# Numerators of linear attention that read the turned rows in storage order, with tokens put in order at the PSUM evacuation and units 8 to 31 begun four steps earlier

## The chip, the core and the metric

One core of a Trainium2 chip runs the whole kernel. The core has five engines with a queue of instructions each: TensorE (PE in the profile; its weight loads are listed as PEld), VectorE (DVE), ScalarE (ACT), GpSimd (POOL) and SyncE (SP), which here only starts transfers. Each engine works through its queue in order, and semaphores let one engine wait for another. SBUF is the working memory, PSUM the memory that TensorE writes its results to, in eight banks.

The metric is device time in microseconds, the median of three runs. All numbers of single instructions come from one profiled execution.

## What is computed

A transformer block on 2048 tokens of width 1024: linear attention with 32 heads of 32 features, then a ReLU MLP of width 3584, both with a layer norm ahead and a residual.

```
pq = einsum(q, w_phi);  pk = einsum(k, w_phi)            # per head, 32 x 32
phi_q = concat(softmax(pq), softmax(-pq));  phi_k likewise   # 64 features
kv  = einsum("bhsf,bhsd->bhfd", phi_k, v)                # 64 x 32 per head
z   = einsum("bhsf->bhf", phi_k)
num = einsum("bhqf,bhfd->bhqd", phi_q, kv)
den = einsum("bhqf,bhf->bhq", phi_q, z) + 1e-6
h   = x + (num / den) @ wo
out = h + relu(layernorm(h) @ w1) @ w2
```

The change lies in `num`, the numerators.

## The kernel before

Everything is float32. The large products split each operand into a high and a low part and take three matmuls (`mm3`, L182 to L184). One such triple is a **step**. Steps are grouped into **items** of eight: a projection of one tile of 128 tokens to 512 columns. Other work is hung on the steps by hand: `when(step, f, ...)` writes the instructions of `f` into the queues right behind that step of TensorE. So the order within each queue is the order of the steps, whatever the engine is doing by then. The splits of weights (`Units.advance`: a copy on ScalarE, L125, then a subtraction on GpSimd or VectorE, L129) go in behind each step when a buffer of the ring is free; the transfers that fetch the weights are queued on SP with them.

The items run in this order: keys and values of the first half of the tokens, queries of the first half, keys and values of the second half (`last_kv` is the last of these), queries of the second half (16 items), then the output projection `wo` (32 items, four groups of tokens), then the MLP. The attention itself runs beside the last queries and the output projection.

**Units.** The queries' exponentials are stored to DRAM (`ed`) and come back as 32 units. A unit is a tile of 128 partitions by 1024 values and holds 256 tokens for a part of the heads. A unit goes through these functions, each at its own offset from the unit's `start`:

- `at_load` (L552, queued on SP): fetches the rows into a `qe` tile, one of six buffers. The buffer is that of the unit six before, whose last reader is that unit's burst of numerators.
- `at_sums` (L595, GpSimd, twice) and `at_reduce` (L602, VectorE, twice): products with `z` and their sums.
- `at_cross` (L613, ScalarE, four small copies), `at_den` (L617 and L618, GpSimd), `at_inverse` (L621, VectorE): the denominators.
- `at_scale` (L631; L626 for the first six units; GpSimd): the rows are divided in place.
- `at_turn` (L637, VectorE): a transpose of every 32 x 32 block in place, so that the features come to lie on the partitions.
- `at_num` (L650, TensorE; on odd units, for two units together): a **burst** of 16 products, each of 64 features by 32 columns of `kvL` with 256 tokens, into two PSUM banks `ac`. The profile lists two matmuls per product. There are 16 bursts.
- right behind it the evacuation: two copies on ScalarE (L657) give the high part of `oT`, and two steps later `at_low` (L667, two subtractions on VectorE) gives the low part. `oT` is the stationary operand of the output projection.

Units 0 to 5 have their denominators made ahead (`early_*`), and only load, scale, turn and numerators at the normal place. Units below 8 are spaced 19/2 steps apart and begin at step 8 (last_kv + 4); from unit 8 on they are 8 steps apart, one unit per item.

After `at_turn` a tile's free dimension is ordered (i, n, c, t): two halves, four blocks `n`, four heads' places `c`, 32 tokens `t`. The token order wanted in `oT` is t outside and n inside. In the kernel before, the matmul's moving operand is read in that order: n innermost, 128 elements apart, then t, then i. What lands in PSUM is then in order and the evacuation reads neighbours.

In the same queues beside the units: the queries' maxima, differences and sums on VectorE (L516, L517, L520, L521, L534, L535), one set per query item; the residual additions (L704, L707) of the output projection; layer-norm statistics (L222, L765); and the splits of `wo` (`w` and `wf` for the two sets of buffers).

Of the kernel before, what the change touches and what calls it, by code (L numbers as in the profile page):

```python
# [140 lines left out]
def kernel(  # L141
# [416 lines left out]
    e_q, ez_of, tz_of, den_of, ph_of, acc_of, phT_of = {}, {}, {}, {}, {}, {}, {}  # L558
# [75 lines left out]
    def at_turn(u):  # L634

        ph = ph_of.pop(u)
        v.transpose(ph, ph)  # L637
        phT_of[u] = ph.rearrange("p (i n c t) -> p c i t n", i=2, n=4, c=4)

    def at_num(u):  # L640


        acc_of[u] = banks = ac_bank(), ac_bank()
        for j in range(2):
            b, q, r = UNITS[u - 1 + j]
            for g in range(2):
                rows = slice(64 * g, 64 * (g + 1))
                for c in range(4):
                    h = 2 * c + r
                    pe.matmul(banks[g][32 * c:32 * (c + 1), 256 * j:256 * (j + 1)],  # L650
                              kvL[rows, 2 * q + h // 4, 32 * (h % 4):32 * (h % 4 + 1)],
                              phT_of[u - 1 + j][rows, c], start=j == 0, stop=j == 1)
        del phT_of[u - 1], phT_of[u]
        if u % 8 == 1:
            oT[b] = opool[b % 2].tile([P, 2, 8, 512], F32R, name="oT")
        for g in range(2):
            act.activation(at_out(u, 0, g), at_in(banks[g]), AF.Copy)  # L657

    def at_in(ps):
        return ps.rearrange("p (u i n) -> p u i n", u=2, i=2)  # L660

    def at_out(u, part, g):
        return oT[u // 8][:, part, u % 8 - 1:u % 8 + 1, :].rearrange("p u (i g n) -> p u i g n", i=2, g=2)[:, :, :, g]

    def at_low(u):
        for g, ps in enumerate(acc_of.pop(u)):
            v.tensor_sub(at_out(u, 1, g), at_in(ps), f32(at_out(u, 0, g)))  # L667

    oT, opool = {}, {}
# [277 lines left out]
    def item(gen, *args, keys):  # L947
        items.append((gen, args + (keys,)))
        steps.extend((k,) for k in keys)
        return len(items) - 1  # L950
# [11 lines left out]
    for b, tiles in enumerate(groups):  # L962
        for hf in range(2):

            pairs = b == 0 and hf == 0
            for j in range(0, 4, 2 if pairs else 1):
# [3 lines left out]
                for half in range(2):  # L970
                    n = item(wo_pair, tiles[j:j + 2], hf, half, keys=[("wo", hf, 4 * half + k // 2) for k in range(8)])
# [26 lines left out]
    def when(step, f, *args):  # L998

        if step < 8 * first_up:  # L1000
            do(step // 8, step % 8, f, *args)
        else:
            do(first_up + (step - 8 * first_up) // 4, step % 4, f, *args)
# [4 lines left out]
    for t in range(1, NT):  # L1008
        n = t - 1 if t < HT else q_n[1, t - HT] + 1
# [42 lines left out]
    last_kv = kv_n[1, 3, NT - 1]  # L1052
# [62 lines left out]
    a0 = last_kv + 6  # L1115
    for (sl, t), n in q_n.items():
# [3 lines left out]
        b, i = place_of[t]  # L1120
# [1 line left out]
            when(8 * n + 34, sm_store, b)  # L1122
            when(8 * n + (48, 48, 48, 72)[b], sm_load, b)
    for u in range(32):
        start = 8 * (a0 + u) if u >= 8 else 8 * (last_kv + 4) + 19 * u // 2
        slack = 6 if u < 6 else 0

        for step, f, *args in ((-5, at_load), (6, at_sums, 0), (10, at_reduce, 0), (9, at_sums, 1), (12, at_reduce, 1),
                               (14, at_cross), (16, at_den), (18, at_inverse), (20, at_scale), (26, at_turn)):
            if u >= EARLY or f in (at_load, at_scale, at_turn):  # L1130
                when(max(start + step, 8 * (last_kv + 4)), f, u, *args)
        if u % 2:
            when(start + 30 + slack, at_num, u)
            when(start + 32 + slack, at_low, u)
        if u < EARLY:
            start = 8 * (kv_n[1, u // 2, NT - 1] + 4) + (-2, 19)[u % 2]
            for step, f in ((0, early_load), (9, early_sums), (14, early_reduce), (17, at_cross), (20, at_den), (22, early_scale)):
                when(start + step, f, u)
# [35 lines left out]
    def up_step(b, p, m):  # L1174

        return up0 + 4 * (up_n[b, p, m] + 1 - first_up)

    for j, m in enumerate(UP):

        for g in range(2):  # L1180
            step = up0 + (8 * j + (-62, -29)[g] if j < 4 else 6 * (j - 4) + 4 + 2 * g)
# [4 lines left out]
            step = up_step(0, NP - 1, m) + 2 * j  # L1186
# [4 lines left out]
    for b in range(2):  # L1191
        for p in range(NP):
            for m, k, f, *args in UP_BESIDE:
                if f is up_store:
                    args = [b, p, *args]
# [7 lines left out]
    for n, (w, p, j) in enumerate((w, p, j) for w in (1, 2) for p in range(NP) for j in range(2)):  # L1203
        step = sums_at[n]
# [7 lines left out]
    for b in range(2):  # L1212
        for m in DOWN:
            n = down_n[b, m, NP - 1] + 1
# [110 lines left out]
```

## Time and profile before

| | |
|---|---|
| median of three runs | 1884.09 us (1883.66 to 1885.63) |
| profiled execution | 1884.29 us, span 1882.5 us |
| TensorE busy | 1871.4 us, 99% of the span |
| VectorE, GpSimd, ScalarE busy | 1067.8, 979.9, 770.9 us |
| granted TensorE clock | 1.0 |
| L650, all bursts | 33.8 us busy, 512 matmuls |
| first and last burst begin at | 551.0 and 763.2 us |

How the rows are read: a row of a group names the line, the engine, the operation, output and inputs by the program's tile names, the shape, and the count. Times in a time line are microseconds from the start of the span, first the start, then the length. Behind a bar stand busy time, the mean of one in ns, and the idle time of the engine just before it with the engine and line that ended it. Matmuls overlap, and their ends are modelled, so the distance between their starts says more than their length. A row with a `64*32` names the rows and columns of the array that the matmul uses.

### The profile page before, as it was taken

The page shows a single profiled execution, that of the slowest core. Times are in us where ns is not written, and L with a number is a line of the kernel's source. Part 1 is how long each engine was busy: PE and PEld are TensorE (multiplying, and loading weights), DVE is VectorE, ACT ScalarE, POOL GpSimd, SP SyncE. Part 2 cuts the span into 40 slices and gives each one's busy share as a digit, 9 for nine tenths or more (in the row PEclk, how much of TensorE's full clock was granted, in tenths as well). Part 3 has the DMA queues.
Part 4 walks back from the last instruction along what each step waited for, and adds up shares of the span by engine and source line. Part 5 has one row for each costly group of instructions (what it writes and reads, how often), then busy time and mean ns, then how long its engine had stood idle before and what let it go on. Part 6 is the DMA issues. An engine that isn't in the chain of part 4 may idle for free.

```text
span 1882.5 us, 28853 instructions
## 1 busy us (share of the span) xinstructions
PE 1871.4 (99%) x10064; PEld 1516.4 (81%) x10064; DVE 1067.8 (57%) x1655; ACT 770.9 (41%) x1379; POOL 979.9 (52%) x991
## 2 busy tenths in 40 slices
PE   9999999999999999999999999999999999999999
PEld 7777788888876677888888888888888888888887
DVE  7787688677689777565555563444433333343333
ACT  5322244233333334355455554444444444444442
POOL 4877745888846979343233222222344444444443
PEclk9999999999999999999999999999999999999999
DMA  7988798666575766787889985666677677767775
GB/s 225 291 284 294 230 292 268 204 192 200 181 222 178 228 222 190 242 288 213 260 256 261 318 275 176 192 191 216 212 236 216 207 226 237 239 214 217 217 215 177
DMA packets 333635, 433.04 MB, mean 230 GB/s; under 512 B 28720, under 2 KB 194608, under 8 KB 333488
## 3 DMA queue, kind: packets, MB, share of 16 engines
q1 hardware_dynamic: 299696, 414.41, 70.2%
q10 hardware_dynamic: 33792, 16.78, 3.1%
q8 instruction: 79, 1.29, 0.3%
q14 instruction: 68, 0.56, 0.1%
HBM read 293.21 MB, written 137.89 MB: 229 GB/s over the span
## 4 chain that ended last, share of the span: by engine, by line
PE 97%; POOL 1%; DVE 1%; issue 0%; DMA 0%; ACT 0%; SPq 0%; DVEq 0%; POOLq 0%
PE mm L182 25%; PE mm L183 25%; PE mm L184 25%; PE ac L182 4%; PE ac L184 4%; PE ac L183 4%; PE tp L184 2%; PE tp L183 2%; PE tp L182 2%; PE ac L650 2%; PE tp L246 1%; PE ac L465 1%; POOL ez L595 0%; PE tp L291 0%; POOL w L129 0%
## 5 line engine op out<-in xcount | busy, mean ns | idle before, releaser
L129 POOL TENSOR_TENSOR w<-raw,w 128x512 fp32r<-128x512 f32 x353 | 469.1, 1331 | 702.3 <-ACT w L125 665.1
L125 ACT ACTIVATE w<-raw 128x512 fp32r<-128x512 f32 x686 | 408.8, 626 | 508.8 <-PE mm L184 235.1
L129 DVE TENSOR_TENSOR w<-raw,w 128x512 fp32r<-128x512 f32 x333 | 271.0, 814 | 513.4 <-ACT w L125 504.8
L182 PE MATMUL mm<-w,xT 128*128 128x512 f32 x768 | 305.4, 398 | 0.0
L183 PE MATMUL mm<-w,xT 128*128 128x512 f32 x768 | 299.8, 390 | 0.4 <-POOL w L401 0.4
L184 PE MATMUL mm<-w,xT 128*128 128x512 f32 x768 | 299.2, 390 | 0.0
L184 PE MATMUL mm<-hT,w 128*128 128x512 f32 x672 | 261.4, 389 | 0.0
L182 PE MATMUL mm<-hT,w 128*128 128x512 f32 x672 | 261.4, 389 | 0.0
L183 PE MATMUL mm<-hT,w 128*128 128x512 f32 x672 | 261.4, 389 | 0.0
L182 PEld LDWEIGHTS mm<-w,xT 128*128 128x128 f32 x768 | 144.1, 188 | 36.7 <-issue 5.5
L363 POOL TENSOR_TENSOR b<-b 128x256 f32<-128x256 f32 x176 | 144.3, 820 | 48.6 <-DMA b<-in_w_dram 37.6
L184 PEld LDWEIGHTS mm<-w,xT 128*128 128x128 f32 x768 | 144.2, 188 | 30.7
L183 PEld LDWEIGHTS mm<-w,xT 128*128 128x128 f32 x768 | 144.3, 188 | 29.2 <-POOL w L401 1.0
L182 PE MATMUL mm<-w 128*128 128x512 f32 x392 | 152.5, 389 | 0.0
L183 PE MATMUL mm<-w 128*128 128x512 f32 x392 | 152.5, 389 | 0.0
L184 PE MATMUL mm<-w 128*128 128x512 f32 x392 | 152.5, 389 | 0.0
L182 PEld LDWEIGHTS mm<-hT,w 128*128 128x128 f32 x672 | 126.1, 188 | 26.3
L183 PEld LDWEIGHTS mm<-hT,w 128*128 128x128 f32 x672 | 126.1, 188 | 26.2
L184 PEld LDWEIGHTS mm<-hT,w 128*128 128x128 f32 x672 | 126.1, 188 | 26.1
L454 POOL TENSOR_TENSOR zacc<-zacc,kphi 128x512 f32<-128x512 f32 x60 | 80.7, 1345 | 10.1 <-DVE kphi L446 10.1
L182 PEld LDWEIGHTS mm<-w 128*128 128x128 f32 x392 | 73.6, 188 | 15.3
L183 PEld LDWEIGHTS mm<-w 128*128 128x128 f32 x392 | 73.6, 188 | 15.3
(173 smaller groups left out, 3119.8 us busy)
## 6 DMA issues: line engine op xcount, KB each, us to landing
raw<-t SPq DMA_DIRECT2D x224, 256.0 KB, 3.8
raw<-ad SPq DMA_DIRECT2D x196, 256.0 KB, 3.0
raw<-in_w_dram SPq DMA_DIRECT2D x168, 256.0 KB, 3.1
ad<-c SPq DMA_DIRECT2D x112, 256.0 KB, 3.6
b<-in_w_dram SPq DMA_DIRECT2D x44, 512.0 KB, 5.5
t<-b SPq DMA_DIRECT2D x44, 512.0 KB, 5.0
ad<-s SPq DMA_DIRECT2D x84, 256.0 KB, 4.0
ed<-qe ACTq DMA_DIRECT2D x64, 256.0 KB, 3.9
```

Of the source, the lines that this page charges most:

```text
L125: nc.scalar.activation(w[:, 0, :], raw[1], AF.Copy)
L129: eng.tensor_tensor(out=w[:, 1, :], in0=raw[1], in1=w[:, 0, :].bitcast(F32), op=ALU.subtract)
L182: pe.matmul(ps, a_hi, b_hi, start=first, stop=False, skip_group_check=more)
L183: pe.matmul(ps, a_hi, b_lo, start=False, stop=False, skip_group_check=more)
L184: pe.matmul(ps, a_lo, b_hi, start=False, stop=last, skip_group_check=more)
L246: pe.transpose(pt[:, k, :], xn[:, (4 * j + k) * P:(4 * j + k + 1) * P], ident)
L363: pool.tensor_tensor(out=tsum[*u, *out], in0=tsum[*u, *a], in1=tsum[*u, *b], op=ALU.subtract)
L454: pool.tensor_tensor(out=zacc[s], in0=zacc[s], in1=phi_of[key], op=ALU.add)
L465: pe.matmul(kv_ps[s][g][32 * i:32 * (i + 1), 0:64], vt[:, 32 * h:32 * (h + 1)], phi[:, 64 * h:64 * (h + 1)], start=first, stop=last)
L650: pe.matmul(banks[g][32 * c:32 * (c + 1), 256 * j:256 * (j + 1)], kvL[rows, 2 * q + h // 4, 32 * (h % 4):32 * (h % 4 + 1)], phT_of[u - 1 + ...
```

## The change

Three things, all in the attention:

1. `at_turn` hands the numerators a view in which the moving operand is read with the 32 tokens `t` innermost, next to each other, and the eight blocks (i and n together) outside, 128 apart. The product's columns then land in PSUM in the order (i, n, t).
2. `at_in` and `at_out`, used by the copies (L657) and the subtractions (L667), read PSUM with n innermost, 32 elements apart, and write `oT` in the order it had before: four blocks by 32 tokens, contiguous runs of 128. What `oT` holds is the same.
3. The start of units 8 to 31 is four steps lower. Their numerators and evacuation get a slack of four, so they stay at the same step. `at_load` moves from 5 to 8 steps ahead of the start, for all units (the earliest ones are held by the lower limit of the schedule).

```diff
         v.transpose(ph, ph)
-        phT_of[u] = ph.rearrange("p (i n c t) -> p c i t n", i=2, n=4, c=4)
+        phT_of[u] = ph.rearrange("p (n c t) -> p c n t", n=8, c=4)
...
     def at_in(ps):
-        return ps.rearrange("p (u i n) -> p u i n", u=2, i=2)
+        return ps.rearrange("p (m n t) -> p m t n", m=4, n=4)
 
     def at_out(u, part, g):
-        return oT[u // 8][:, part, u % 8 - 1:u % 8 + 1, :].rearrange("p u (i g n) -> p u i g n", i=2, g=2)[:, :, :, g]
+        return oT[u // 8][:, part, u % 8 - 1:u % 8 + 1, :].rearrange("p u (i g t n) -> p g (u i) t n", i=2, g=2, n=4)[:, g]
...
     for u in range(32):
-        start = 8 * (a0 + u) if u >= 8 else 8 * (last_kv + 4) + 19 * u // 2
-        slack = 6 if u < 6 else 0
+        start = 8 * (a0 + u) - 4 if u >= 8 else 8 * (last_kv + 4) + 19 * u // 2
+        slack = 6 if u < 6 else 4 if u >= 8 else 0
 
-        for step, f, *args in ((-5, at_load), (6, at_sums, 0), (10, at_reduce, 0), (9, at_sums, 1), (12, at_reduce, 1),
+        for step, f, *args in ((-8, at_load), (6, at_sums, 0), (10, at_reduce, 0), (9, at_sums, 1), (12, at_reduce, 1),
                                (14, at_cross), (16, at_den), (18, at_inverse), (20, at_scale), (26, at_turn)):
```

## The prediction

> **What bounds the kernel.** I read the page first, then TensorE's waits, then the line that the change rewrites, then the queues of VectorE and GpSimd around it.
>
> ```profile
> span 1882.5 us, 28853 instructions
> PE 1871.4 (99%) x10064; PEld 1516.4 (81%) x10064; DVE 1067.8 (57%) x1655; ACT 770.9 (41%) x1379; POOL 979.9 (52%) x991
> PE 97%; POOL 1%; DVE 1%; issue 0%; DMA 0%; ACT 0%; SPq 0%; DVEq 0%; POOLq 0%
> ```
>
> TensorE is busy for 99% of the span, and 97% of the chain that ended last runs through it. So a microsecond counts only if TensorE's own work shrinks, or one of its few waits goes or comes.
>
> ```profile
> PE ac L650 <- DVE qe L637: 1.9, 1, 1.9
> PE mm L183 <- DVE w L129: 1.1, 1, 1.1
> ```
>
> These two waits lie in the attention stage. The first is a burst of numerators (L650) that waits for the turned rows of its second unit; the second is an output projection that waits for a split weight. The change has two handles, then: what a burst costs on TensorE, and when the turned rows are ready.
>
> **What a burst costs.** Sixteen bursts run, one per pair of units. The rows give shortest, median and longest ns of a matmul by line.
>
> ```profile
> L650 PE MATMUL ac<-qe,kvL x512: 610/627/707, 551.0 to 764.7; 64*32 64x256 f32 x171
> L291 PE MATMUL mm<-wt,wphi x224: 371/374/398, 40.3 to 200.5; 32*32 32x256 f32 x112
> ```
>
> Both stream 256 float32 columns through small tiles of the array. L650 reads its moving rows with the four blocks `n` innermost, 128 elements apart; L291, in the weight fold, reads eight runs of 32 neighbours, 128 apart. That is exactly the pattern that L650 has after the change. It takes 374 ns against 627. A burst and a fold in order of time (start, length, group):
>
> ```profile
> 550.42 0.39 PE L183 MATMUL mm<-w,xT 128*128 128x512 f32 x1
> 550.65 0.39 PE L184 MATMUL mm<-w,xT 128*128 128x512 f32 x1
> 550.97 0.71 PE L650 MATMUL ac<-qe,kvL 64*32 64x256 f32 x8
> 551.44 0.71 PE L650 MATMUL ac<-qe,kvL 64*32 64x256 f32 x8
> 551.89 0.70 PE L650 MATMUL ac<-qe,kvL 64*32 64x256 f32 x8
> 552.33 0.70 PE L650 MATMUL ac<-qe,kvL 64*32 64x256 f32 x8
> 552.96 0.50 PE L182 MATMUL mm<-w,xT 128*128 128x512 f32 x1
> ...
> 199.38 0.45 PE L291 MATMUL tp<-wt,wphi 32*32 32x256 f32 x8
> 199.62 0.42 PE L291 MATMUL tp<-wt,wphi 32*32 32x256 f32 x8
> 200.03 0.50 PE L291 MATMUL tp<-wt,wphi 32*32 32x256 f32 x8
> ```
>
> L650 goes in four rounds of eight tiles, 0.45 us apart (550.97, 551.44, 551.89, 552.33), and the next projection starts 0.63 after the last: 1.99 in all. The fold's second round of the same tiles starts 0.24 after the first. With that spacing three rounds take 0.72; the last one shortens by the difference of the durations, 0.63 - 0.25 = 0.38. A burst then takes 1.10 and saves 0.89 us. Bounds: the fold's third round comes 0.41 after its second (200.03 - 199.62), where it goes to other weights and other columns; with one such step, at the change from one unit to the next, a burst saves only 0.72. At best rounds follow like the projection's matmuls, 0.23 apart: 0.92. I take 0.89, because L650's rounds before show no longer step at that place (0.45 like the others). Sixteen bursts: 14.2 us (11.5 to 14.7). The 0.32 between a projection and a burst (550.65 to 550.97) stays.
>
> **Evacuation.** Each burst is copied out by two ScalarE and two VectorE instructions. They now read PSUM in steps of 32 elements and write runs of 128; no row of before reads PSUM so.
>
> ```profile
> L657 ACT ACTIVATE oT<-ac x32: 590/596/601, 553.1 to 765.8; 128x512 fp32r<-128x512 f32 x32
> L667 DVE TENSOR_TENSOR oT<-ac,oT x32: 628/681/694, 554.3 to 766.6; 128x512 fp32r<-128x512 f32 x32
> L637 DVE STREAM_TRANSPOSE qe<-qe 128x1024 f32<-128x1024 f32 x32 | 39.2, 1224 | 4.3 <-POOL qe L626 2.4 <-POOL qe L631 1.8
> L781 DVE STREAM_TRANSPOSE y<-xin 128x1024 f32<-128x1024 f32 x4 | 8.1, 2031 | 1.2 <-DMA raw<-t 1.2
> ```
>
> The nearest row of a stepped access on VectorE is L781, a transpose that writes every fourth element: 2031 ns against 1224 for L637, which writes neighbours, 1.66 times. TensorE's own ratio is 627/374 = 1.68. Lower bound: no change, since writes stay in runs and reads were at their best. I take no change. A fold round gives 256 float32 columns in 0.24 us, 0.94 ns each, twice the 0.45 of a projection's column (0.23 for 512), as if TensorE streamed each column twice. A stepped round of 0.45 us is then 0.9 ns a read, while L667 takes 681/512 = 1.33 ns an element, so a stepped read need not be its limit. (If each column is read only once, a stepped read is 1.8 ns, and the upper end is near.) Upper end: 1.66 times, 0.45 us more per instruction.
>
> [...]
>
> **Who covers what.** From unit 8 on, all that a unit issues moves four steps up, 4 x 0.68 = 2.7 us (a step is three matmuls 0.23 apart): on GpSimd two products, two denominator steps and the scaling; on VectorE two sums, a reciprocal and the turn; on ScalarE four small copies. The row load moves seven steps up (three for earlier units). Numerators and evacuation stay in place. In stretches (busy us and count of PE, PEld, DVE, ACT, POOL, then clock and DMA):
>
> ```profile
> 565.00:581.00 16.00, 16.00 (x95) 11.91 (x93) 15.76 (x26) 5.18 (x13) 9.96 (x13) 1.00 0.58 180
> 581.00:592.00 11.00, 11.00 (x72) 7.80 (x71) 10.68 (x17) 3.21 (x4) 6.72 (x10) 1.00 0.44 126
> 592.00:611.00 19.00, 17.87 (x100) 12.78 (x99) 17.18 (x27) 8.34 (x19) 15.14 (x17) 1.00 0.65 197
> 624.00:640.00 16.00, 14.13 (x90) 9.50 (x97) 13.24 (x18) 6.01 (x18) 15.84 (x14) 1.00 0.67 216
> 681.00:707.00 26.00, 26.00 (x161) 18.91 (x160) 19.57 (x30) 6.56 (x21) 19.20 (x22) 1.00 0.82 263
> ```
>
> VectorE is 98% full from 565 to 592, GpSimd 99% from 624 to 640; by 681 both have a quarter free. So the seven bursts up to 641 gain only what these queues let through, and the nine behind keep theirs: 9 x 0.89 = 8.0 us.
>
> The first seven, in order. The fourth burst (units 6 and 7):
>
> ```profile
> 590.88 1.19 DVE L637 STREAM_TRANSPOSE qe<-qe 128x1024 f32<-128x1024 f32 x1
> 591.99 0.64 DVE L602 TENSOR_REDUCE qtz<-ez 128x16 f32<-128x512 f32 x1
> ...
> 592.38 2.08 PE L650 MATMUL ac<-qe,kvL 64*32 64x256 f32 x32
> ```
>
> Unit 7's turn ends at 592.07, in a full queue that faster reads don't shorten, and unit 8's second sum (0.6) now stands ahead of it: 592.67. TensorE comes 3 x 0.89 = 2.67 sooner, at 589.71, and wants unit 7 two rounds later, at 590.19. It waits 2.5 us. What is kept: 4 x 0.89 - 2.5 = 1.06.
>
> ```profile
> 610.38 0.50 PE L183 MATMUL mm<-w,oT 128*128 128x512 f32 x1 [1.13 <-DVE w L129]
> ...
> 624.37 1.18 PE L650 MATMUL ac<-qe,kvL 64*32 64x256 f32 x16
> 627.42 1.21 PE L650 MATMUL ac<-qe,kvL 64*32 64x256 f32 x16 [1.87 <-DVE qe L637]
> ...
> 630.81 1.30 POOL L129 TENSOR_TENSOR wf<-raw,wf 128x512 fp32r<-128x512 f32 x1
> 633.46 0.39 PE L182 MATMUL mm<-wf,oT 128*128 128x512 f32 x1
> ```
>
> The projection's wait of 1.13 at 610: a sum of unit 10 (0.6) moves ahead of the split on VectorE and TensorE comes 1.06 sooner, up to 2.8 if the queue doesn't move, nothing if it does; I leave it at 1.13. The fifth burst adds 0.89: 1.95. The sixth (units 10, 11) starts its second half at 627.42 instead of 624.37 + 0.92, a wait of 2.13. TensorE gets there 1.95 + 0.44 = 2.39 sooner, so unit 11 would have to be 4.5 sooner; four steps give 2.7, and 1.8 of wait remains. Kept: 1.95 + 0.89 + 2.13 - 1.8 = 3.2. Then the split that GpSimd ends at 632.11 is wanted at 633.46, 1.35 later; with TensorE 3.2 sooner and one more unit product ahead of it (1.3, the length of this split) the wait lies between nothing and 3.1; I take half, 1.6. With the seventh burst 1.6 + 0.89 = 2.5 us is kept at 641.
>
> **The row load.**
>
> ```profile
> SPq L552 <- PE ac L650: 36.6, 9, 13.1
> ...
> DMA to landing us min/median/max: 2.6/5.2/6.9
> ```
>
> From unit 14 on an even unit's load stands two steps ahead of the burst that frees its buffer, so SP waits there about 2 x 0.68 + 1.1 us, with loads and stores of the residual behind it that have more than ten steps to their use. SP waits like this already (36.6 us, nine times) with no wait on TensorE. The data is wanted 14 steps, 9.5 us, after the load's place; 2.5 + 5.2 fits, 2.5 + 6.9 is right at it and would cost GpSimd, which has room there. Nothing.
>
> **Sum.** 8.0 + 2.5 = 10.5 us. The profiled execution took 1884.29 us (0.2 over the median of the three runs, 1884.09): 1873.8.
>
> **Rivals.**
> 1. *The queues don't hold TensorE*: the loads and splits that they wait for also come sooner, all bursts keep 0.89 and both waits go: 14.2 + 1.1 + 2.1 = 17.4, 1866.9. For it: GpSimd has 3.9 us idle between 592 and 611. Against it: VectorE at 98%.
> 2. *Stepped PSUM reads are slow, 1.66 times*: 0.9 us more on VectorE per burst. It hurts where that queue is full, behind six of the first seven bursts: 5.4 lost, 1879.2. [...]
> 3. *They are so slow that VectorE sets the pace*, the other side. It decides where 12 instructions eat 10.5 us, 0.88 each, from 2.3 times on. At three times (2.04 us) they add 12 x 1.36 = 16.3: 5.8 slower, 1890.1. Nothing in before excludes it; no row shows more than 1.68.
> 4. *The reads are no faster*, because the burst's pace has another cause (two row groups in one bank pair, say): only the sixth burst's 2.1 goes, 0.6 comes back at a split: 1882.8, no measurable change. Against it: the row of L291.
>
> **Chances.** Forecast 0.58, rival 1 0.09, rival 2 0.15, rival 4 0.07, rival 3 0.11. So faster by over 0.2% (3.8 us, about what a measurement here can tell) 0.82, within it 0.07, slower 0.11. The range leaves out rivals 3 and 4: 1867 from rival 1 to 1880.5 just past rival 2. The forecast's own range is 1870 to 1877.5: from two thirds of rival 1's extra kept, to nothing kept before 641 and bursts that save only 0.72.
>
> **What would show it.** L650's median near 374 ns and a burst without a wait at 1.1 us from its first matmul to the next projection: the reads. L657 and L667 still at 596 and 681 ns: the evacuation. A wait of TensorE on L637 at the fourth burst, the sixth burst's wait smaller, waits on splits (L129) near 610 and 632: the queues. Bursts from 652 on without waits, in 13.1 - 0.9 us from one to the next: the kept gain. I would be wrong if L667 grows, if waits show up behind 652, or if L650 stays above 600 ns.

## The result and the profile after

The kernel with the change takes 1872.29 us (median of four runs, 1870.48 to 1872.47), the kernel before 1884.07 beside it. The ratio is 0.9934 with the interval 0.9917 to 0.9951: 11.8 us faster. The profiled execution of after is the shortest of the four, 1870.48 us. It is some 1.8 us better than the other three, and the stages below add up to its time, not to the median; the experiment on the loads takes that difference up.

The page of after, first lines and the chain by engine:

```profile
span 1868.7 us, 28840 instructions
PE 1856.5 (99%) x10064; PEld 1516.3 (81%) x10064; DVE 1063.8 (57%) x1655; ACT 770.5 (41%) x1379; POOL 979.0 (52%) x991
...
PE 93%; DVE 3%; POOL 1%; issue 1%; ACT 0%; DMA 0%; SPq 0%; ACTq 0%; DVEq 0%; POOLq 0%
```

TensorE is still busy 99% of the span, 14.9 us less in sum (1871.4 - 1856.5). The chain has 3% of VectorE in it where before had 1%: some of its new waits run through VectorE's queue. The changed lines, by line (shortest, median, longest ns):

```profile
L650 PE MATMUL ac<-qe,kvL x512: 375/376/632, 550.5 to 751.1; 64*32 64x256 f32 x171
L657 ACT ACTIVATE oT<-ac x32: 579/596/619, 551.7 to 752.0; 128x512 fp32r<-128x512 f32 x32
L667 DVE TENSOR_TENSOR oT<-ac,oT x32: 622/676/693, 553.5 to 752.8; 128x512 fp32r<-128x512 f32 x32
```

A matmul of the numerators went from 627 to 376 ns, and the two evacuation instructions stayed what they were (596 against 596, 676 against 681). The first burst in order of time:

```profile
550.48 1.09 PE L650 MATMUL ac<-qe,kvL 64*32 64x256 f32 x32
551.50 0.50 PE L182 MATMUL mm<-w,xT 128*128 128x512 f32 x1
```

From its first matmul to the next projection it takes 551.50 - 550.48 = 1.02 us, where before took 1.99: 0.97 saved. All bursts but the fourth and the sixth take 1.02 to 1.03.

To see where the gain is kept, I set the same burst's times in the two traces beside each other and took away the 0.49 us by which the first burst begins sooner (551.0 and 550.48 from the start of each span, before anything of the change acts).

| TensorE ahead of before, us | predicted | measured |
|---|---|---|
| after the third burst | 2.67 | 3.00 |
| after the fourth | 1.06 | 0.91 |
| ahead of the fifth | 1.06 | 1.45 |
| after the fifth | 1.95 | 2.64 |
| after the sixth | (3.2) | 5.14 |
| ahead of the seventh (behind the wait on the split) | 1.6 | 3.34 |
| after the seventh | 2.5 | 4.41 |
| after the sixteenth | 10.5 | 13.31 |

TensorE's waits in the attention stage of after (total, times, longest), and the two smaller ones in order of time, at the sixth burst and at the split of GpSimd:

```profile
PE ac L650 <- DVE qe L637: 2.8, 2, 2.4
...
PE mm L183 <- POOL wf L129: 1.5, 1, 1.5
```

```profile
622.35 0.67 PE L650 MATMUL ac<-qe,kvL 64*32 64x256 f32 x16 [0.45 <-DVE qe L637]
...
629.73 0.50 PE L183 MATMUL mm<-wf,oT 128*128 128x512 f32 x1 [1.46 <-POOL wf L129]
```

The largest is at the fourth burst, in order of time:

```profile
588.90 0.66 PE L650 MATMUL ac<-qe,kvL 64*32 64x256 f32 x16
591.94 1.11 PE L650 MATMUL ac<-qe,kvL 64*32 64x256 f32 x16 [2.38 <-DVE qe L637]
592.98 0.80 PE L182 MATMUL mm<-w,xT 128*128 128x512 f32 x1
593.57 0.63 PE L183 MATMUL mm<-w,xT 128*128 128x512 f32 x1
594.00 0.63 PE L184 MATMUL mm<-w,xT 128*128 128x512 f32 x1
```

The first half runs, the second waits for unit 7's turn. VectorE meanwhile:

```profile
588.59 0.68 DVE L602 TENSOR_REDUCE qtz<-ez 128x16 f32<-128x512 f32 x1
589.18 1.21 DVE L534 TENSOR_REDUCE qsm<-qe 128x32 f32<-128x1024 f32 x1
590.43 0.35 DVE L535 RECIPROCAL qsm<-qsm 128x32 f32<-128x32 f32 x1
590.70 1.19 DVE L637 STREAM_TRANSPOSE qe<-qe 128x1024 f32<-128x1024 f32 x1
```

It has no gap: a sum of unit 8 (L602, moved up), a query item's sum, then the turn, which ends at 591.89. TensorE starts again at 591.94. Something follows that I had not foreseen. The projections behind come 0.43 us apart (593.57 to 594.00) instead of 0.23. The stretches behind the wait (busy us and count of PE, PEld, DVE, ACT, POOL, then granted clock, DMA share, GB/s):

```profile
591.00:593.00 2.00, 1.06 (x17) 0.25 (x17) 2.00 (x4) 0.33 (x1) 1.87 (x2) 0.65 0.37 101
593.00:595.00 2.00, 2.00 (x12) 1.61 (x6) 2.00 (x5) 1.60 (x3) 1.41 (x2) 0.50 0.60 161
595.00:597.00 2.00, 2.00 (x10) 1.63 (x9) 2.00 (x5) 1.26 (x5) 2.00 (x2) 0.99 0.00 0
```

The granted clock is 0.50 until 595 (I call this half clock below). The burst's second half takes 1.04 us to the next projection (592.98 - 591.94) where it takes 0.57 in the first burst, and from 592.98 to 594.85 the projections run at half pace: 0.47 + 0.94, about 1.4 us lost beside the wait itself.

### The profile page after: what moved, and what is told of

Its sections match the earlier page's. It is cut to its first block, busy times and chain, and to the rows that moved or that the text cites. A ratio compares the mean times of both kernels' runs of the same rounds, so it can differ in the third digit from the quotient of the medians.

```text
span 1868.7 us, 28840 instructions
## 1 busy us (share of the span) xinstructions
PE 1856.5 (99%) x10064; PEld 1516.3 (81%) x10064; DVE 1063.8 (57%) x1655; ACT 770.5 (41%) x1379; POOL 979.0 (52%) x991
## 3 DMA queue, kind: packets, MB, share of 16 engines
q8 instruction: 79, 1.29, 0.3%
## 4 chain that ended last, share of the span: by engine, by line
PE 93%; DVE 3%; POOL 1%; issue 1%; ACT 0%; DMA 0%; SPq 0%; ACTq 0%; DVEq 0%; POOLq 0%
PE mm L182 24%; PE mm L183 24%; PE mm L184 24%; PE ac L182 4%; PE ac L184 4%; PE ac L183 4%; PE tp L184 2%; PE tp L183 2%; PE tp L182 2%; PE tp L246 1%; PE ac L465 1%; PE ac L650 1%; DVE qsm L534 0%; DVE qe L637 0%; POOL w L129 0%
## 5 line engine op out<-in xcount | busy, mean ns | idle before, releaser
L125 ACT ACTIVATE w<-raw 128x512 fp32r<-128x512 f32 x686 | 409.4, 626 | 508.8 <-PE mm L184 232.4
L183 PEld LDWEIGHTS mm<-w 128*128 128x128 f32 x392 | 73.6, 188 | 15.3
L184 PEld LDWEIGHTS mm<-w 128*128 128x128 f32 x392 | 73.6, 188 | 15.2
L182 PEld LDWEIGHTS mm<-w 128*128 128x128 f32 x392 | 73.6, 188 | 15.3
```

Of the source, the lines that this page charges most:

```text
L125: nc.scalar.activation(w[:, 0, :], raw[1], AF.Copy)
L182: pe.matmul(ps, a_hi, b_hi, start=first, stop=False, skip_group_check=more)
L183: pe.matmul(ps, a_hi, b_lo, start=False, stop=False, skip_group_check=more)
L184: pe.matmul(ps, a_lo, b_hi, start=False, stop=last, skip_group_check=more)
```

## The experiments

Theory: faster reads save about 0.97 us a burst; what is lost of it before 641 is lost to VectorE's full queue (fourth burst) and GpSimd's (sixth burst, split). Rivals: the units begun sooner bring the gain; a better order of the queues would bring the lost part back; the stepped PSUM reads or the moved loads cost something.

**The reads alone.** Units and loads at the steps of before.

```diff
-        start = 8 * (a0 + u) - 4 if u >= 8 else 8 * (last_kv + 4) + 19 * u // 2
-        slack = 6 if u < 6 else 4 if u >= 8 else 0
+        start = 8 * (a0 + u) if u >= 8 else 8 * (last_kv + 4) + 19 * u // 2
+        slack = 6 if u < 6 else 0
...
-        for step, f, *args in ((-8, at_load), (6, at_sums, 0), (10, at_reduce, 0), (9, at_sums, 1), (12, at_reduce, 1),
+        for step, f, *args in ((-5, at_load), (6, at_sums, 0), (10, at_reduce, 0), (9, at_sums, 1), (12, at_reduce, 1),
```

> Parts one and two alone: the numerators read runs of 32 and the evacuation puts the tokens in order, all units at their old steps and loads. Theory (the queues of VectorE and GpSimd hold TensorE up to 641): a burst without a wait takes 1.02 us as after the change, 16 x 0.97 = 15.5 us less work, but unit 11 and the units about it are no sooner, so the sixth burst waits longer than its 2.1 us of before, and the fourth, fifth or seventh wait too; 6 to 8 us faster, 1876 to 1878. Rival (the shorter bursts are the whole gain, the four steps do nothing): 1872, waits as after the change.

Measured: 1875.48 us against 1884.81, ratio 0.9953 (0.9939 to 0.9968). That is 9.3 us faster where 6 to 8 was expected, half a microsecond below the expected times; in the trace TensorE ends 8.6 us ahead. The waits that came up:

```profile
PE ac L650 <- DVE qe L637: 3.1, 4, 1.3
PE ac L650 <- POOL ez L595: 1.8, 1, 1.8
PE mm L183 <- DVE w L129: 1.8, 1, 1.8
```

Five bursts wait (the fourth takes 3.10 us, the fifth 1.87, the sixth 2.51, the seventh 2.10, the fourteenth 1.87). The split's wait of 1.8, just ahead of the fifth burst, is followed by half clock too, from 611.6 to 615. Without the earlier units the faster TensorE waits at five bursts, but most of the gain is the reads'.

**The earlier units alone.** The kernel before with the start, slack and load step of after.

```diff
-        start = 8 * (a0 + u) if u >= 8 else 8 * (last_kv + 4) + 19 * u // 2
-        slack = 6 if u < 6 else 0
+        start = 8 * (a0 + u) - 4 if u >= 8 else 8 * (last_kv + 4) + 19 * u // 2
+        slack = 6 if u < 6 else 4 if u >= 8 else 0
```

> Part three alone: units from the ninth on four steps sooner and the loads sooner, reads and evacuation as before. Theory: only the sixth burst's wait of 2.1 us goes and the fourth or a split gives back some tenths: 1 to 2.5 us faster, 1881.5 to 1883, no change that can be measured; bursts stay at 1.99 us. Rival (the earlier start is what frees the attention stage): at least 4 us faster, under 1880.

Measured: 1881.64, ratio 0.9983 (0.9973 to 0.9992), 3.2 us faster; 3.0 in the trace. More than the 1 to 2.5 that was expected, because not only the sixth burst's wait is gone but the projection's at 610 as well. Bursts take 1.98 to 2.03 throughout, and one wait comes in:

```profile
PE mm L183 <- POOL wf L129: 0.7, 1, 0.7
```

So this part is worth a third of the other. Both alone give 8.6 + 3.0 = 11.6 in the traces and 12.5 in the medians, together 13.3 and 11.8. So nothing large comes from doing both together.

**The fourth burst six steps later.** If the fourth burst's wait of 2.5 us is a loss by order alone, then asking for units 6 and 7 six steps later should bring it back.

```diff
-        slack = 6 if u < 6 else 4 if u >= 8 else 0
+        slack = 6 if u < 8 else 4
```

> The changed kernel with the numerators of units 6 and 7 (the fourth burst) six steps later. Theory: the burst finds its turned rows, so its wait of 2.5 us and the half clock behind it (about 1 us) go, but VectorE is as full as it was, so the weight splits of the first output projections (near 600 to 608) come no sooner and TensorE waits there instead, 2 to 3.5 us: 1870 to 1872.5. Rival (the wait at the fourth burst is a cost by itself): 3.5 us under the changed kernel, about 1868.7, no new waits near 600 to 608.

Measured: 1873.18, ratio 0.9938 (0.9924 to 0.9953), 0.9 us slower than after and 0.7 above the expected range. The fourth burst waits no more and takes 1.03 us. But the projections behind it do:

```profile
603.29 0.50 PE L183 MATMUL mm<-w,oT 128*128 128x512 f32 x1 [0.77 <-DVE w L129]
606.28 0.50 PE L184 MATMUL mm<-w,oT 128*128 128x512 f32 x1 [1.11 <-DVE oT L667]
609.11 0.80 PE L182 MATMUL mm<-w,oT 128*128 128x512 f32 x1 [1.63 <-ACT w L125]
610.90 0.80 PE L183 MATMUL mm<-w,oT 128*128 128x512 f32 x1 [1.00 <-DVE w L129]
```

Four waits, 4.5 us where 2 to 3.5 was expected, and half clock for 6.8 us from 609. Three of them are for VectorE, one for a copy on ScalarE. So this order doesn't bring the loss back: TensorE meets the work that VectorE still owes at the next things that it needs. One order is not all orders. VectorE stands idle here for 1.45 us at 600, behind a ScalarE copy (L125), so a better order may exist; none was tried.

**Less work on VectorE.** The maximum and the minimum over a query item (L516, L517) read 8 of the 32 features for the second half of the tokens; the softmax stays the same, only its guard against large exponents is weaker.

```diff
+        part = pq[:, :, 0:8] if t >= HT else pq
-        v.tensor_reduce(out=m[:, 0, :], in_=pq, op=ALU.max, axis=AX.X)
-        v.tensor_reduce(out=m[:, 1, :], in_=pq, op=ALU.min, axis=AX.X)
+        v.tensor_reduce(out=m[:, 0, :], in_=part, op=ALU.max, axis=AX.X)
+        v.tensor_reduce(out=m[:, 1, :], in_=part, op=ALU.min, axis=AX.X)
```

> The changed kernel with VectorE relieved: the maximum and minimum that shift the query softmax are taken over 8 of the 32 features for the tokens of the second half (the softmax is the same in exact arithmetic, only less guarded against overflow), about 0.35 us less for each of two reductions, 0.7 us per query item, over 5 us by the fourth burst. Theory (VectorE's full queue holds the fourth burst and the first splits): the wait at the fourth burst falls under 0.3 us, the clock stays at 1.0 behind it, and 3 us or more are gained: 1866 to 1869.5. Rival (GpSimd's products and scalings hold the turned rows, or the loads do): the wait stays at 2 us or more, and the time within 1 us of the changed kernel.

Measured: 1867.33, ratio 0.9907 (0.9893 to 0.9922), 5.0 us faster than after (3.6 in the traces, where after's is its short execution). The groups of one of the two reductions (busy, mean ns, idle before) and the stretch in which after waited and ran at half clock:

```profile
L517 DVE TENSOR_REDUCE qmx<-mm 128x16 f32<-128x512 f32 x16 | 10.9, 682 | 8.1 <-PE mm L184 8.1
L517 DVE TENSOR_REDUCE qmx<-mm 128x16 f32<-128x128 f32 x16 | 4.5, 283 | 9.8 <-PE mm L184 9.8
```

```profile
588.00:596.00 8.00, 8.00 (x63) 5.83 (x62) 7.93 (x15) 5.94 (x13) 7.26 (x10) 1.00 0.35 102
```

Each query item costs VectorE 0.8 us less (twice 682 - 283 ns). The fourth burst takes 1.08 us, TensorE is busy all 8 us, and the clock stays at 1.00: without the wait there is no half clock here. TensorE is 3.91 ahead after the fourth burst and 5.39 ahead of the fifth, where after had 0.91 and 1.45. The difference of 3.0 at the fourth burst is the wait of 2.56 (the third round of products at 591.94 instead of 589.14 + 0.24) and 0.47 of the clock. The one of 3.9 ahead of the fifth holds the other 0.94.

**Moving rows at steps of 1, 2, 4, 8, 16 and 128, burst by burst.** After, with other orders of the matmul's reads, and the PSUM reads of before.

```diff
-        phT_of[u] = ph.rearrange("p (n c t) -> p c n t", n=8, c=4)
+        k = (1, 2, 4, 8, 16, 32)[u // 2 % 6]
+        phT_of[u] = ph.rearrange("p (i n c t) -> p c i t n", i=2, n=4, c=4) if k == 32 else \
+            ph.rearrange("p (n c b a) -> p c n a b", n=8, c=4, a=k)
```

> The changed kernel with the moving rows of the numerators read in other orders, the burst deciding: the innermost elements lie 1, 2, 4, 8 or 16 apart (then the rest of each run of 32, then the blocks), and in every sixth burst 128 apart as before the change; the evacuation reads neighbours as before, so tokens come out in another order (what is left out is the ordering of the tokens). [...] Rival that any step costs: 2 is as slow as 128. Rival that only long distances cost (other banks or rows of the memory): 2, 4, 8 and 16 stay near 376 ns. Evacuation: ScalarE 596 and VectorE 676 to 681 ns as with the stepped reads of the changed kernel.

Measured in one execution (1876.03 us). Bursts in order of time, at steps of 2, 8, 16, 128 and 1:

```profile
648.29 1.17 PE L652 MATMUL ac<-qe,kvL 64*32 64x256 f32 x32
...
675.43 2.04 PE L652 MATMUL ac<-qe,kvL 64*32 64x256 f32 x32
688.50 1.30 PE L652 MATMUL ac<-qe,kvL 64*32 64x256 f32 x32
700.84 2.06 PE L652 MATMUL ac<-qe,kvL 64*32 64x256 f32 x32
715.77 1.09 PE L652 MATMUL ac<-qe,kvL 64*32 64x256 f32 x32
```

| innermost step (elements) | places read in turn | matmul, median ns | burst to next projection, us |
|---|---|---|---|
| 1 | 32 neighbours | 376 | 1.02 |
| 2 | 16, then the 16 between | 392 | 1.10 |
| 4 | 8 | 634 | 2.00 |
| 8 | 4 | 632 | 1.97 |
| 16 | 2 | 429 | 1.23 |
| 128 (before) | 4 | 622 | 1.99 |

So the pace depends on the read order, the only thing that differs between these bursts (rival 4 would have had them all alike). It falls into two groups, and not by the length of the step: 4, 8 and 128 are slow (622 to 634 ns), 2 is fast (392), and 16 is nearly as fast (429), where the reads go to and fro between two places 64 bytes apart. Both rivals of this expectation fall: not every step costs (392 ns at 2 against 622 at 128), and not only long distances do (634 and 632 ns at 4 and 8). What makes an order slow, the runs don't say.

The evacuation of this kernel, which reads neighbours in PSUM:

```profile
L659 ACT ACTIVATE oT<-ac 128x512 fp32r<-128x512 f32 x32 | 17.4, 595 | 37.0 <-PE ac L652 37.0
L669 DVE TENSOR_TENSOR oT<-ac,oT 128x512 fp32r<-128x512 f32 x32 | 20.3, 675 | 7.7 <-ACT oT L659 7.6
```

Means of 595 and 675 ns with neighbours, 596 and 673 with steps of 32 elements in after: these stepped PSUM reads cost the two engines nothing.

**What slow evacuations would have cost.** Rival 2's price, put on VectorE by hand: each subtraction of the evacuation is done twice, 1.2 us more per burst.

```diff
-            v.tensor_sub(at_out(u, 1, g), at_in(ps), f32(at_out(u, 0, g)))
+            for _ in range(2):
+                v.tensor_sub(at_out(u, 1, g), at_in(ps), f32(at_out(u, 0, g)))
```

> The changed kernel with each VectorE subtraction of the evacuation done twice (same result), 1.2 us more on VectorE per burst: what a slow read of PSUM would have cost. Theory (the queue is full behind six of the first seven bursts and has room later): 6 x 1.2 = 7.2 us lost at the most, 1877 to 1880, lost before 641, none after. Rival (VectorE sets the pace throughout): 16 x 1.2 = 19 us lost, 1891. Rival (VectorE's fullness costs TensorE nothing): 1872 to 1873.

Measured: 1879.1, ratio 0.997 (0.9958 to 0.9982), 6.8 us slower than after. The two traces lie further apart, 8.5 us at the last burst. Of this 6.9 is lost up to the end of the seventh burst (2.46 behind before, where after was 4.41 ahead), nearly all at one place: the fourth burst takes 7.08 us instead of 4.08, and 3.2 more go on the way to the fifth, where half clock lasts twice as long (to 599.6) and two splits are waited for (0.7 and 1.3).

```profile
594.99 1.11 PE L650 MATMUL ac<-qe,kvL 64*32 64x256 f32 x16 [5.37 <-DVE qe L637]
```

Most of the rest, 1.5, is lost between the fourteenth and the fifteenth burst, where none was expected: TensorE waits 1.29 us there for a layer-norm copy on ScalarE (L248). The doubled subtractions as its cause are not shown; a smaller wait of the same kind comes and goes in other variants.

**The loads back at their old steps.** After, with the row loads as many steps ahead of their use as in before.

```diff
-        for step, f, *args in ((-8, at_load), (6, at_sums, 0), (10, at_reduce, 0), (9, at_sums, 1), (12, at_reduce, 1),
+        for step, f, *args in ((-1 if u >= 8 else -5, at_load), (6, at_sums, 0), (10, at_reduce, 0), (9, at_sums, 1), (12, at_reduce, 1),
```

> The changed kernel with the row loads of all units back at the steps of before (units from the ninth on still start four steps sooner). Theory (loads are never what a unit waits for here): the time of the changed kernel within 1 us. Rival (the earlier loads carry the gain of the earlier start): GpSimd waits for rows and 2 us or more are lost, 1874.5 or more.

Measured: 1872.43, ratio 0.9935 (0.992 to 0.995), the median of after. So the place of the loads is worth nothing that these runs can show. This kernel's profiled execution (1872.08) shows what the three other runs of after may look like, since the profiled one of after was 1.6 us shorter than this. The fourth burst waits the same (2.38 in both rows), but the half clock lies later:

```profile
593.00:595.00 2.00, 2.00 (x8) 1.53 (x7) 2.00 (x5) 1.25 (x3) 1.85 (x2) 0.63 0.60 162
595.00:597.00 2.00, 2.00 (x7) 1.56 (x6) 2.00 (x5) 1.25 (x5) 2.00 (x4) 0.52 0.25 13
```

It costs about the same, but in after it began at 591.6 and so covered the burst's second half, here it began behind it, at 593.5. So here the evacuation copies on ScalarE start 0.43 us sooner (592.65 against 593.08), the weight copy behind them too, and GpSimd's queue, in the same order, runs up to 0.46 sooner. Then the same split on VectorE takes twice as long. VectorE and GpSimd around 598, in after and in this kernel:

```profile
598.27 0.63 DVE L129 TENSOR_TENSOR w<-raw,w 128x512 fp32r<-128x512 f32 x1
598.17 1.87 POOL L595 TENSOR_TENSOR ez<-qe,zb 128x512 f32<-128x512 f32 x1
```

```profile
598.28 1.28 DVE L129 TENSOR_TENSOR w<-raw,w 128x512 fp32r<-128x512 f32 x1
597.71 1.30 POOL L595 TENSOR_TENSOR ez<-qe,zb 128x512 f32<-128x512 f32 x1
598.97 1.74 POOL L129 TENSOR_TENSOR w<-raw,w 128x512 fp32r<-128x512 f32 x1
```

In after the split keeps its 0.63 and GpSimd's product takes 1.87 instead of 1.30, 0.57 longer, though its start is recorded 0.10 sooner than the split's (times on GpSimd are rough). In this kernel the product is under way, the split takes 1.28, and its end, 599.56, is 0.55 behind the product's at 599.01, as if it had waited for it. Then GpSimd's next split takes 1.74, 0.45 over its usual 1.29. The other four VectorE splits up to 610 (600.75 and 606.51 in after, 601.42 and 608.14 here) also start while a GpSimd instruction runs and end 0.54 to 0.56 behind it. That one of the two engines is served and the other waits is my reading of these lengths; no row shows a cause, and the starts of the first pair, 0.10 us apart, don't settle which came first. The three splits on VectorE from 598 to 610 take 0.63 + 1.11 + 0.75 = 2.49 us in after, 1.28 + 2.07 + 1.76 = 5.11 here. VectorE has 0.15 us idle in between, so the last one ends at 609.90, 2.64 later than in after, and TensorE waits for it 0.99 us:

```profile
609.96 0.50 PE L183 MATMUL mm<-w,oT 128*128 128x512 f32 x1 [0.99 <-DVE w L129]
```

That is the projection's wait of before at 610, and the prediction had left it standing. It is there in this kernel and the next, not in the profiled execution of after. That the unprofiled runs of after have it is likely, not shown.

**Units 12 to 31 only two steps sooner.** GpSimd's split near 629 waits behind unit products; with later units less far ahead it might not.

```diff
-        start = 8 * (a0 + u) - 4 if u >= 8 else 8 * (last_kv + 4) + 19 * u // 2
-        slack = 6 if u < 6 else 4 if u >= 8 else 0
+        sooner = 4 if u < 12 else 2
+        start = 8 * (a0 + u) - sooner if u >= 8 else 8 * (last_kv + 4) + 19 * u // 2
+        slack = 6 if u < 6 else sooner if u >= 8 else 0
```

> The changed kernel with units 8 to 11 four steps sooner but units 12 to 31 only two. Theory (unit products that the change moves ahead of the last weight splits on GpSimd cost TensorE the wait near 628): that wait of 1.6 us shrinks to under 0.5, the other waits stay: 1870.5 to 1872. Rival (the wait there is only GpSimd's total work): no change, 1872 to 1873.

Measured: 1872.26, ratio 0.9935 (0.9918 to 0.9951); above the expected range, and the same as after. The sixth burst's wait went (the burst takes 1.03 us), but the split's stayed at 1.0 us, where less than 0.5 was expected. Yet the order of GpSimd's queue is not without effect. Beside the kernel with the loads back, whose waits are the same up to the fifth burst, one unit product stands behind the split instead of ahead of it. The split ends 1.26 us sooner (630.06 against 631.32), and ahead of the seventh burst TensorE is 1.23 further (2.94 against 1.71 ahead of before). Between the fourteenth and the fifteenth 1.2 is lost again, at a wait of 1.00 for a layer-norm copy on ScalarE (L248). Whether the later units cause that wait is not shown.

**Both queues relieved.** The kernel with shorter maxima, and the six splits of `wo` that use the second set of buffers all on VectorE (three of them are GpSimd's in after).

```diff
+            odd = odd or key[0] == "wo" and key[1] == 1 and key[2] > 1
```

> The changed kernel with the query maxima and minima over 8 features as above, and the six splits of the far output weights all on VectorE (three of them were on GpSimd, 1.3 us each). Theory (between 597 and 640 GpSimd is the queue that holds the sixth burst and the last splits, once VectorE has room): the two waits there, 0.8 and 1.6 us, fall under 0.5 in sum: 1865 to 1866.3. Rival (VectorE, not GpSimd, holds these too): waits stay or grow, 1867 or more.

Measured: 1865.28, ratio 0.9896 (0.988 to 0.9913): faster than before by 19.9 us and than after by 7.0. The waits of TensorE on turns and splits in the attention are gone from the list; the sixth and the seventh burst still take 0.3 and 0.2 us more than the others. All that is left in the whole profile:

```profile
PE tp L247 <- ACT xn L240: 1.6, 1, 1.6
PE tp L1246 <- POOL ones L1242: 1.6, 1, 1.6
PE tp L247 <- ACT xin L249: 0.4, 1, 0.4
PE mm L184 <- POOL w L402: 0.4, 1, 0.4
```

TensorE is 10.3 us ahead of before after the seventh burst and 18.5 after the last. That is about the sum of everything the change could give: 16 x 0.97 = 15.5 from the reads and 3.3 from the two waits of before.

## Why the prediction was right

1873.8 was forecast, 1872.29 measured, and the forecast's own range (1870 to 1877.5) holds it. (By the range's own terms its ends come to 1869.2 and 1877.8.) The mechanism was right in the main. That the sum before 641 came out so close is in part luck: a loss by the clock that it didn't have stands against waits that became shorter (at the sixth burst) or went (at 610). By its steps:

- **What a burst saves**: right in kind, a little too small. 0.89 was taken, 0.97 measured, 15.5 instead of 14.2 for sixteen. The rounds come 0.24, 0.22 and 0.21 apart, so the three steps take 0.67 and not 0.72, and the last one needs 0.35 instead of 0.38. The feared step of 0.41 at the change of units isn't there. The row of the fold (374 ns) gave the duration to 2 ns (376).
- **The evacuation**: right at no change: 596 and 673 ns stepped, 595 and 675 with neighbours. Rivals 2 and 3 fall with it. Rival 2's way of pricing came out in size only: e_low2 lost 6.8 us for 1.2 us more per burst, where six bursts at 1.2 make 7.2. But the loss wasn't paid burst by burst; its trace has it in the wait at the fourth burst, the clock behind it and the next splits. Rival 3's pace was not reached by any run.
- **The nine bursts behind 641**: right. 8.0 was forecast, 13.31 - 4.41 = 8.9 measured, which is nine times 0.97 and a rest of 0.2; no wait appears there.
- **The fourth burst**: the wait of 2.5 was right (2.56 by the rounds), in place and cause. What was missing is the half clock behind it, 1.4 us. The 0.91 measured after this burst against 1.06 predicted hides two errors that nearly cancel: 0.4 more from four bursts and 0.47 less by the clock.
- **The wait at 610**: "I leave it at 1.13" failed for the profiled execution, where it is gone, and holds in the variants with the loads back and with units two steps sooner (1.0). In the two traces laid beside each other it goes with which of VectorE's split and GpSimd's product is drawn out at 598 (0.63 and 1.87 us in after, 1.28 and 1.30 with the loads back), and that with 0.4 us by which the place of the half clock moves the evacuation. No step of the prediction had this.
- **The sixth burst**: 1.8 of its wait was to remain, 0.69 did (the burst takes 1.70 instead of 1.02). Its step reckoned that unit 11's turn comes only the four steps, 2.7 us, sooner. Its work is hung on TensorE's steps, and TensorE was 2.64 ahead by then; with both the turn could come 5.3 sooner, and the second half of the burst, which waits for it, began 4.6 sooner (627.42 to 622.35, less 0.49). What rival 1 said of the queues is right at this place. This term is 1.1 us off.
- **GpSimd's split near 630**: 1.6 forecast between 0 and 3.1, 1.80 lost (5.14 to 3.34).
- **The sum up to 641**: 2.5 forecast, 4.41 measured in the profile: 0.6 from seven bursts, 1.1 from the sixth's wait, 1.5 at the place of the one at 610 (0.91 to 1.45, with 0.94 of the clock added back), against it 1.4 of the clock and 0.2 of the split; the 0.3 left over is what the fifth and the seventh burst of before took beyond 1.99 (2.21 and 2.10). In the profile with the loads back it was 2.78, so the median's gain of 11.8 is nearer to the forecast than the profiled run's.
- **The row load**: right at nothing (1872.43 with the old places).

Rival 1 (queues don't hold, 1866.9) fell by the fourth burst's wait; the one other order that was tried (e_late4) doesn't give it back. With the queues relieved by hand (e_far) its time was reached and passed. Rival 4 fell by the steps experiment. What stays open is why three runs of after are 1.8 us longer than its profiled one: the later half clock and the wait at 610, which the profiles of the two variants with the same time have (loads back, units two steps sooner), are the likely cause.

## What to carry to other kernels

Before reordering a matmul's operand somewhere downstream, look for another matmul in the same trace that already reads in the new order: its duration was right to 2 ns here, and the cost of undoing the order at the PSUM evacuation was zero. When the engine that bounds a kernel gets faster, go through the queues of the others stage by stage and find the full ones (98 and 99% here): there, moving one wait to another step moved the loss, and taking work out of the full queues (0.8 us per item, then three splits) brought back 7 us. Price the waits on TensorE with the clock behind them: 2.4 us at one place cost another 1.4 here, and three shorter waits close together (0.77, 1.11 and 1.63 us, the fourth burst six steps later) came with half clock for 6.8 us.

## What the runs showed of the hardware

- **Half clock after a short wait.** A wait of 2.38 us in the fourth burst (2.56 by the rounds) was followed by a granted clock of 0.50 for 3.4 us: from 591.6 to 595 in after, where it begins inside the wait, from 593.5 to 597 with the loads back. In before the sixth burst waited 2.13 us by the rounds and the clock stayed at 1.00. In e_low2 a wait of 5.4 us brought 0.50 from 593 to 599.6. Where the drop begins varies from run to run (by 1.9 us here, at the same wait of 2.38).
- **Shorter waits close together were followed by it too.** In after the clock drops at 591.61 and is back at 595.03, 3.41 us later. In the 3.41 us ahead of the drop TensorE was idle for 2.05 us in after, for 1.75 in e_reads (drop at 611.64) and for 2.2 in e_late4 (drop at 609), there with no single wait over 1.63. Yet before has 1.87 us of idle time in its sixth burst's wait (0.93 in each of the two rows below, 3.41 - 2.48) and keeps 1.00. So idle time within 3.41 us does not settle it alone; what else counts these runs don't show. The rows (busy us and count of PE, PEld, DVE, ACT, POOL, then granted clock, DMA share, GB/s) of before, then the 3.41 us ahead of the drop in e_reads:

```profile
623.08:626.49 3.41, 2.48 (x23) 0.96 (x21) 3.41 (x4) 2.19 (x7) 3.41 (x5) 1.00 0.70 269
626.49:629.90 3.41, 2.48 (x22) 1.30 (x23) 2.65 (x4) 2.00 (x4) 3.33 (x5) 1.00 1.01 260
```

```profile
608.23:611.64 3.41, 1.66 (x34) 0.66 (x34) 2.98 (x5) 1.45 (x6) 2.42 (x2) 1.00 1.03 297
```

- **Reads alternating between two places are nearly fast.** A step of 16 elements with two places in turn takes 429 ns, four places 8 apart 632.
- **A split on VectorE may cost two or three times as much.** Of the six splits from 598 to 610 in two traces (after and the loads back), the same 128x512 subtraction takes 0.63 to 2.07 us; the five over 0.63 start while GpSimd is in an instruction and end 0.54 to 0.56 us behind it; the one of 0.63 is recorded 0.10 us behind the start of one, which then takes longer (1.87 instead of 1.30). In a full queue that is enough to make or unmake a wait of TensorE (0.99 us at 610).
